# Two orders in a gated linear-attention and S4D kernel: where the output weights are split, and k's sum behind q's clamp

## The chip, the cores and the metric

The kernel runs on one core of one Trainium2 chip. The metric is the device time of one execution in microseconds (us). A core has five engines that run side by side, each through its own queue in order: TensorE (PE, matmuls; its weight loads are listed as PEld), VectorE (DVE), ScalarE (ACT), GpSimd (POOL) and SyncE (SP, which here issues all transfers). They wait for one another by semaphores. SBUF is the on-chip memory of 128 partitions, PSUM the small memory with eight banks into which PE writes.

## The reference

For x of 2048 x 448 it mixes two branches with a gate taken from x. Branch a is linear attention with 16 heads of 28; branch b is a long convolution (an S4D kernel) over the sequence:

```python
g = sigmoid((x * gate_w).sum(-1, keepdims=True))
q, k, v = split(x @ wqkv)                                # 16 heads of 28
phi = lambda t: where(t > 0, t + 1, exp(t)) + 1e-6
kv = einsum("bhsd,bhse->bhde", phi(k), v)
z = phi(k).sum(over s)
o = einsum("bhqd,bhde->bhqe", phi(q), kv) / (einsum("bhqd,bhd->bhq", phi(q), z) + 1e-6)
a = o @ wo
K = 2 * einsum("dn,dnl->dl", C, exp(A * dt * l)).real    # A, C, dt from the parameters
b = causal_conv(x, K) + x * D_skip
out = g * a + (1 - g) * b
```

## The kernel before, in words

The sequence is cut into 16 chunks of 128 rows. The kernel has a head (chunks 0 and 1, while the weights arrive), a main loop over `c` = 1 to 13, a tail for the last two chunks, and a second loop that makes the output chunk by chunk. The order of the instructions on each engine is the order in which the program issues them; nothing reorders them.

Products are made in a form of fp32 that the array takes in one pass (`F32R`), so each operand is split into a high part (a copy that rounds) and a low part (the difference, helper `low`, line 266), and each product is made of high x high, high x low and low x high. The output weights `wo` are split too, in two halves of two column blocks each: one ACT copy makes the high part of a half (L718), two POOL subtractions make the low parts. They are read only in `mrows` (L894), after the main loop.

One pass of the main loop, in the order of PE's work: k's projection of chunk c + 1 (11 matmuls into the bank `k`, or `v0` for c = 2 and 4), the convolution's running sums `v` of one or two earlier chunks (`do_v`, two matmuls each, which read the x tile and `w`), q's projection of chunk c (11 matmuls into the one bank `q`), and `do_g` for chunk c (11 matmuls of phi(k) with x). Around it:

- `split_next`: ACT copies x of chunk c + 2 (L273), POOL makes its low parts (L266, two instructions), `skip` multiplies x by D_skip on POOL (L288).
- k's features of chunk c + 1: two ACT passes (`k_exp`, L418 and L419), DVE's maximum in the bank (`k_max`, L422), ACT's high part (`k_high`, L430), DVE's low part (`k_low`, L437), and DVE's running sum over the chunks `zb` (`k_sum`, L433).
- q's features of chunk c: ACT's exponentials (`q_exp`, L450 to L456), DVE's maximum (`q_max`, L464) and ACT's final sum, which writes `pq` (`q_add`, L468). For chunk 2 alone the clamp is done in two DVE instructions, `q_max` L461 and L462, and the second writes `pq` itself.
- the convolution's rows: `do_w1` (L510), `do_w2` (L515), `v_post` (L525) and `v_add` (L533) on DVE, `v_row` on ACT (L529) and SP.
- `drip` puts the small steps of the S4D preparation (`s4d_prepare`) between them in passes 1 to 5; at c = 5 eight small transposes of its result (L380) run on PE.

Behind the loop, `z_products` (L555) multiplies the collected rows on DVE, then come the features of chunk 15, the sum of `zb` over the partitions on PE (L749 to L751), and from it POOL's first products of the second part (`norm_a`, L766).

The lines at stake in the main loop are these:

```python
        k_low(c + 1)
        k_sum(c + 1)
...
            q_exp(c, project(c, wqh, wql, D + 2, "q"))
            q_max(c)
...
            q_add(c)
        drip(c, 2)
        if c in (NC - 6, NC - 4):
...
        if c == NC - 6:
...
        do_g(c)
```

Of the kernel before, what the change touches and what calls it, by code (L numbers as in the profile page):

```python
# [8 lines left out]
F32R = mybir.dt.float32r  # L9
# [8 lines left out]
D = 448  # L18
# [3 lines left out]
NC = S // P  # L22
J = 4
DJ = D // J
# [155 lines left out]
def gated_mix_kernel(ctx: ExitStack, tc: tile.TileContext, xin, wv_d, wo_d, abc_d, ldt_d, dsk_d,  # L180
                     first_d, tri_d, ident_d, mask_d, gcat_d, sel_d, nabc_d, nldt_d, xrev_d, lag_d, out):
    nc = tc.nc
    PE, ACT, DVE, POOL, SP = nc.tensor, nc.scalar, nc.vector, nc.gpsimd, nc.sync
# [19 lines left out]
    wo = const.tile([DJ, J, D], F32, name="wo")  # L203
# [19 lines left out]
    xs = work.enter_context(tc.tile_pool(name="xs", bufs=LAG + 4))  # L223
# [9 lines left out]
    def load_x(c):  # L233
        xr[c] = pf[:, 4 * D:4 * D + XC] if c == 3 else xp.tile([P, XC], F32, name="xr", tag="xr")
        if c > 1:
            SP.dma_start(out=xr[c], in_=xin[c])
# [28 lines left out]
    def low(eng, o, r, h):  # L265
        eng.tensor_tensor(out=o, in0=r, in1=h.bitcast(F32), op=ALU.subtract)  # L266

    def split_x(c):
        r = xr[c]
        w = xs.tile([P, XW], F32R, name="xw", tag="x")  # L270
        h, l = xh[c], xl[c] = w, w[:, LT:]
        if c > 1:
            ACT.copy(h[:, :XC], r)  # L273
# [13 lines left out]
    def skip(c):  # L287
        POOL.tensor_tensor(out=y[:, c], in0=xr[c][:, NAT:LO], in1=dsk, op=ALU.mult)  # L288
# [4 lines left out]
    def low_rest(c):  # L293
        low(POOL, xh[c][:, XC:LT], xr[c][:, NAT:LO], xh[c][:, NAT:LO])
# [91 lines left out]
    def pieces(c, wh, wl, n, tag):  # L386
        o = ps.tile([P, 512], F32, name=tag, tag=tag)
        h, l = xh[c], xl[c]
        seq = [(h[:, :P], wh[:, 0])]
        lows = [(l[:, :P], wh[:, 0])]  # L390
        for k in range(1, 4):
            xk = slice(k * P, (k + 1) * P)
            seq += [(h[:, xk], wh[:, k]), (h[:, xk], wl[:, k])]
            lows.append((l[:, xk], wh[:, k]))
        seq += lows

        def run(count):
            for _ in range(min(count, len(seq))):
                a, b = seq.pop(0)
                run.n += 1  # L400
                PE.matmul(o[:, :n], lhsT=a, rhs=b, start=run.n == 1, stop=not seq)  # L401
        run.n = 0
        return o, run

    def project(*args, **kw):
        o, run = pieces(*args, **kw)
        run(11)
        return o
# [6 lines left out]
    def k_exp(c, o):  # L415
        e = pke[c] = tp.tile([P, D], F32, name="e", tag="e")
        pks[c] = o[:, :D]
        ACT.activation(e, pks[c], AF.Relu, scale=-1.0)  # L418
        ACT.activation(e, e, AF.Exp, scale=-1.0)  # L419

    def k_max(c):
        DVE.scalar_tensor_tensor(out=pks[c], in0=pks[c], scalar=1.0, in1=pke.pop(c), op0=ALU.add, op1=ALU.max)  # L422
# [5 lines left out]
    def k_high(c):  # L428
        pkh[c] = tp.tile([P, D], F32R, name="pkh", tag="pkh")
        ACT.add(pkh[c], pks[c], 1e-6)  # L430

    def k_sum(c):
        DVE.scalar_tensor_tensor(out=zb, in0=pks[c], scalar=1e-6, in1=zb, op0=ALU.add, op1=ALU.add)  # L433
# [24 lines left out]
    def q_max(c):  # L458
        if 1 < c < QL:
            e = qe.pop(c)  # L460
            DVE.tensor_scalar(out=e, in0=e, scalar1=1.0, scalar2=1e-6, op0=ALU.min, op1=ALU.add)  # L461
            DVE.scalar_tensor_tensor(out=pq[:, c], in0=qs.pop(c), scalar=C1, in1=e, op0=ALU.add, op1=ALU.max)  # L462
            return
        DVE.scalar_tensor_tensor(out=qs[c], in0=qs[c], scalar=1.0, in1=qe.pop(c), op0=ALU.add, op1=ALU.max)  # L464

    def q_add(c):
        if c >= QL or c < 2:
            ACT.add(pq[:, c], qs.pop(c), 1e-6)  # L468
# [39 lines left out]
    def do_w1(c):  # L508
        v = vt[c] = ps.tile([P, 512], F32, name="v", tag="v%d" % (c % 2))[:, :D]
        DVE.scalar_tensor_tensor(out=v, in0=xh[c][:, NAT:LO].bitcast(F32), scalar=-1.0, in1=slope, op0=ALU.mult,  # L510
                                 op1=ALU.mult)

    def do_w2(c):
        w = wt[c] = tp.tile([P, D], F32R, name="w", tag="w")
        DVE.tensor_tensor(out=w, in0=vt[c], in1=xh[c][:, XC:LT].bitcast(F32), op=ALU.add)  # L515

    def do_v(c):
        for n, w in enumerate((xh[c][:, NAT:LO], wt.pop(c))):
            PE.matmul(vt[c], lhsT=tri, rhs=w, start=n == 0, stop=n == 1)  # L519

    def v_post(c):
        t = vt[c]
        if c == NC - 1:
            vt[c] = tp.tile([P, D], F32, name="t", tag="v0")
        DVE.tensor_tensor(out=vt[c], in0=t, in1=near, op=ALU.mult)  # L525

    def v_row(c):
        r = tp.tile([P, D], F32, name="ut", tag="v0")
        ACT.copy(r[96:], vt.pop(c)[96:])  # L529
        SP.dma_start(out=u[c:c + 1], in_=r[P - 1:P])  # L530

    def v_add(c):
        DVE.tensor_tensor(out=y[:, c], in0=y[:, c], in1=vt[c], op=ALU.add)  # L533

    prep = s4d_prepare()
    def steps(n):
        for _ in range(n):
            next(prep, None)
# [3 lines left out]
    def drip(c, i):  # L542
        if (c, i) == (2, 2):
            ACT.copy(tri, trir)
        steps(DRIP.get((c, i), 0))
# [82 lines left out]
    woh, wol = [], []  # L628
    for c in range(1, NC - 2):
        if c == 1:  # L630
            load_x(4)
            gcr = tp.tile([P, D], F32, name="gcr", tag="w")[:KZ, :2 * RX].rearrange("p (g m) -> p g m", g=2)
            for o, i in ((mask, mask_d), (gcr, gcat_d), (sel, sel_d)):
                SP.dma_start(out=o, in_=i)
        elif c + 3 < NC:
            load_x(c + 3)
        if c == 4:
            SP.dma_start(out=wv, in_=wv_d)
            SP.dma_start(out=wo, in_=wo_d)
        ko, k_run = pieces(c + 1, wkh, wkl, D, "v0" if c in (2, 4) else "k")  # L640
        k_run(KA)
        if c == LAG + 2:
            steps(1)
        k_run(11)

        def split_next():
            if c + 2 < NC:
                split_x(c + 2)
                low(POOL, xl[c + 2], xr[c + 2][:, :NAT], xh[c + 2][:, :NAT])
                if c > 1:  # L650
                    low_rest(c + 2)
                    skip(c + 2)

        if c not in (2, LAG + 2):
            split_next()
        drip(c, 0)
        k_exp(c + 1, ko)
        if c == 2:
            split_next()
        if c == 1:  # L660
            skip(1)
            low_rest(2)
            skip(2)
            low_rest(3)
            skip(3)
        now = vq[:]
        for n in now:
            do_v(n)
        for n in now[:1]:
            v_post(n)  # L670
            v_add(n)
        if c == LAG + 2:
            now = [vs.pop(0)]
            do_w1(0)
            do_w2(0)
        k_max(c + 1)
        if c == LAG + 2:
            steps(1)
        drip(c, 1)
        k_high(c + 1)  # L680
        if c == 1:
            for n in range(2):
                q_add(n)
            steps(1)
        for n in now[1:]:
            v_post(n)
        k_low(c + 1)
        k_sum(c + 1)
        for n in now[1:]:
            v_add(n)  # L690
        if c:
            vq = [vs.pop(0) for _ in range(1 + (c + 1 in TWICE))] if c > LAG + 1 else []
        if c > LAG + 2:
            for n in vq:
                do_w1(n)
        if c > 1:
            q_exp(c, project(c, wqh, wql, D + 2, "q"))
            q_max(c)
        if c == LAG + 2:
            do_v(0)  # L700
            split_next()
            v_post(0)
            v_add(0)
            for n in vq:
                do_w1(n)
        if c > LAG + 1:
            for n in vq:
                do_w2(n)
        for n in now:
            v_row(n)  # L710
        if c > 1:
            q_add(c)
        drip(c, 2)
        if c in (NC - 6, NC - 4):
            wos = xs.tile([DJ, 2, 2, D], F32R, name="wos", tag="x")
            woh.append(wos[:, 0])
            wol.append(wos[:, 1])
            ACT.copy(woh[-1], wo[:, 2 * len(woh) - 2:2 * len(woh)])  # L718
        if c == NC - 6:
            for j in range(2):  # L720
                low(POOL, wol[0][:, j], wo[:, j], woh[0][:, j])
        do_g(c)
        if c == LAG:
            POOL.tensor_copy(gcat, gcr)
# [5 lines left out]
    do_v(NC - 1)  # L730
    zr = z_products()
    v_post(NC - 1)
    for j in range(2):
        low(POOL, wol[1][:, j], wo[:, 2 + j], woh[1][:, j])
    POOL.memset(rows[DT:RX, :RG * P], 0.0)
    k_max(NC - 1)
    k_sum(NC - 1)
# [370 lines left out]
```

## Time and profile before

| what | value |
|---|---|
| median of 3 runs | 182.28 us (182.15 to 182.75) |
| the profiled execution | 182.17 us, its span 180.4 us |
| PE busy | 173.8 us (96%) |
| PE weight loads busy | 154.8 us (86%) |
| DVE, ACT, POOL busy | 133.5, 118.8 and 99.6 us (74, 66 and 55%) |
| mean granted TensorE clock | 0.994 |

How to read the lines shown further on. A line of an engine's timeline has the start from the beginning of the span and the duration in us, the engine, the line of the kernel (a helper's own line where a helper issues it), the operation, out<-in by the program's names, shapes and how many instructions were merged into the row; in square brackets stands the idle time before it and the instruction whose end is taken to have ended that. A line of the waits has the waiting instruction, what it waited for, the total in us, how often, and the longest. The chain that ended last is listed as start, duration and what it was. Matmuls overlap: the row of one is longer than the distance to the next. A DVE or POOL instruction that is held back by something other than a semaphore shows as a longer row, not as idle time.

### The profile page before, as it was taken

The numbers are of one execution on the slowest core, as the hardware profiler recorded it, in microseconds if no ns is written. First come the engines' busy times: TensorE is split into PE (matmuls) and PEld (weight loads), VectorE is DVE, ScalarE is ACT, GpSimd is POOL, SyncE is SP. The second block draws the span as 40 slices with busy tenths as digits, with TensorE's granted clock in tenths as the row PEclk, the third lists the DMA queues.
The fourth block names the chain that finished last, engine by engine and source line by source line (L and its number), as shares of the span: only waits on it lengthen the run. The fifth ranks groups of instructions, "written<-read, shape, count | busy, mean of one in ns | idle before, by whom it ended". The sixth has DMA issues, their size and how long they took to land.

```text
span 180.4 us, 2797 instructions
## 1 busy us (share of the span) xinstructions
PE 173.8 (96%) x894; PEld 154.8 (86%) x894; DVE 133.5 (74%) x264; ACT 118.8 (66%) x255; POOL 99.6 (55%) x95
## 2 busy tenths in 40 slices
PE   6999999999999999999999999999999999999991
PEld 6699997998988888898987999979999989899990
DVE  2885358765977799889879789867898798977440
ACT  4799578585756567675586876384675766765630
POOL 1059959852087347173465719739778767864000
PEclk9999999999999999999999999999999999999997
DMA  6999991890011303213030300000001212213222
GB/s 178 339 347 291 226 311 52 340 275 0 0 59 62 117 1 116 68 53 119 0 117 3 122 0 0 8 16 7 1 0 52 106 52 103 102 52 110 102 83 82
DMA packets 8388, 18.37 MB, mean 102 GB/s; under 512 B 1772, under 2 KB 5728, under 8 KB 8144
## 3 DMA queue, kind: packets, MB, share of 16 engines
q1 hardware_dynamic: 8368, 18.14, 31.1%
q8 instruction: 9, 0.15, 0.3%
q14 instruction: 11, 0.09, 0.2%
HBM read 14.28 MB, written 3.67 MB: 100 GB/s over the span
## 4 chain that ended last, share of the span: by engine, by line
PE 59%; DVE 12%; ACT 10%; DMA 9%; issue 4%; SPq 2%; POOL 1%; DVEq 0%
PE a L837 20%; PE q L401 10%; PE g L504 9%; PE k L401 6%; DMA xr<-in 6%; PE tr L815 4%; DMA y<-in 3%; PE v L519 3%; PE m L894 2%; ACT xw L273 2%; DVE v L510 2%; DVE zb L433 2%; SPq L243 2%; ACT pkh L430 2%; DVE k L422 2%
## 5 line engine op out<-in xcount | busy, mean ns | idle before, releaser
L266 POOL TENSOR_TENSOR xw<-xr,xw 128x448 fp32r<-128x448 f32 (+1 forms) x28 | 34.5, 1252 | 37.3 <-ACT xw L273 24.5
L504 PE MATMUL g<-pkh,xw 128*128 128x448 f32 x112 | 35.6, 366 | 0.0
L401 PE MATMUL q<-wqh,xw 128*128 128x450 f32 x112 | 32.4, 369 | 0.4 <-DVE pq L462 0.4
L401 PE MATMUL k<-wkh,xw 128*128 128x448 f32 x96 | 27.6, 368 | 0.0
L837 PE MATMUL a<-wkh,th 128*128 128x448 f32 (+1 forms) x119 | 26.9, 365 | 0.0
L504 PE MATMUL g<-pkl,xw 128*128 128x448 f32 x64 | 23.5, 367 | 0.0
L504 PEld LDWEIGHTS g<-pkh,xw 128*128 128x128 f32 x112 | 21.1, 188 | 2.6
L401 PEld LDWEIGHTS q<-wqh,xw 128*128 128x128 f32 x112 | 20.9, 188 | 2.5 <-ACT xw L273 0.8
L837 PEld LDWEIGHTS a<-wkh,th 128*128 128x128 f32 x119 | 20.6, 190 | 1.3
L766 POOL TENSOR_TENSOR prod<-pq,zb 128x448 f32<-128x448 f32 x16 | 18.6, 1164 | 4.0 <-ACT zb L752 3.1
L787 POOL TENSOR_TENSOR pn<-pq,den 128x448 f32<-128x448 f32 x16 | 15.1, 945 | 9.9 <-DVE den L778 7.3
L401 PEld LDWEIGHTS k<-wkh,xw 128*128 128x128 f32 x96 | 17.9, 188 | 1.9 <-issue 0.3
L288 POOL TENSOR_TENSOR y<-xr,rows 128x448 f32<-128x448 f32 x15 | 17.5, 1165 | 0.0
L273 ACT CAST xw<-xr 128x1024 fp32r<-128x1024 f32 x13 | 13.6, 1044 | 3.2 <-PE v L519 1.7
L401 PE MATMUL q<-wql,xw 128*128 128x450 f32 x42 | 15.5, 368 | 0.0
L842 DVE SCALAR_TENSOR_TENSOR ot<-y,og,a 128x448 f32<-128x448 f32 (+1 forms) x17 | 10.5, 619 | 6.7 <-PE a L837 6.6
L819 ACT CAST th<-tr 128x512 fp32r<-128x512 f32 x16 | 9.4, 587 | 8.7 <-PE tr L815 8.5
L468 ACT ACTIVATE pq<-q 128x448 f32<-128x448 f32 x13 | 7.1, 545 | 12.0 <-DVE q L464 10.4
L820 DVE TENSOR_TENSOR th<-tr,th 128x512 fp32r<-128x512 f32 x16 | 11.0, 686 | 4.0 <-ACT th L819 3.9
L430 ACT ACTIVATE pkh<-k 128x448 fp32r<-128x448 f32 x13 | 7.1, 544 | 10.0 <-DVE k L422 7.7
L510 DVE SCALAR_TENSOR_TENSOR v<-xw,rows 128x448 f32<-128x448 f32 x16 | 10.8, 703 | 3.3 <-ACT ru L382 2.1
L401 PE MATMUL k<-wkl,xw 128*128 128x448 f32 x36 | 13.2, 367 | 0.0
(184 smaller groups left out, 372.7 us busy)
## 6 DMA issues: line engine op xcount, KB each, us to landing
xr<-in SPq DMA_DIRECT2D x13, 512.0 KB, 4.9
out<-ot SPq DMA_DIRECT2D x15, 224.0 KB, 1.9
pq<-in SPq DMA_DIRECT2D x2, 896.0 KB
y<-in SPq DMA_DIRECT2D x4, 225.0 KB
wv<-in SPq DMA_DIRECT2D x1, 896.0 KB
wo<-in SPq DMA_DIRECT2D x1, 784.0 KB
y<-in SPq DMA_DIRECT2D x3, 224.0 KB, 4.2
xr<-in SPq DMA_DIRECT2D x2, 256.0 KB
```

Source lines behind the costliest of these rows:

```text
L266: eng.tensor_tensor(out=o, in0=r, in1=h.bitcast(F32), op=ALU.subtract)
L273: ACT.copy(h[:, :XC], r)
L288: POOL.tensor_tensor(out=y[:, c], in0=xr[c][:, NAT:LO], in1=dsk, op=ALU.mult)
L401: PE.matmul(o[:, :n], lhsT=a, rhs=b, start=run.n == 1, stop=not seq)
L430: ACT.add(pkh[c], pks[c], 1e-6)
L504: PE.matmul(g[i][:a.shape[1], :D], lhsT=a, rhs=b, start=c == 0 and n == 0, stop=c == NC - 1 and end)
L510: DVE.scalar_tensor_tensor(out=v, in0=xh[c][:, NAT:LO].bitcast(F32), scalar=-1.0, in1=slope, op0=ALU.mult, op1=ALU.mult)
L766: POOL.tensor_tensor(out=pd[c], in0=pq[:, c], in1=zb, op=ALU.mult)
L787: POOL.tensor_tensor(out=hd(n[:, :D]), in0=hd(pq[:, c]), in1=dn[c // 2][:, c % 2, :, None].to_broadcast([P, H, DH]), op=ALU.mult)
L820: DVE.tensor_tensor(out=l, in0=ov, in1=h.bitcast(F32), op=ALU.subtract)
L837: PE.matmul(a[:, lo:hi], lhsT=u_, rhs=w_[:, lo:hi], start=n == 0, stop=n == 10)
L842: DVE.scalar_tensor_tensor(out=ot[:, lo:hi], in0=y[:, c, lo:hi], scalar=og[:, c:c + 1], in1=a[:, lo:hi], op0=ALU.mult, op1=ALU.add)
```

## The change

Two orders are changed; no instruction is added or removed.

- In pass c = 2, `k_sum` of chunk 3 is issued behind `q_max` of chunk 2 instead of ahead of q's projection. On DVE, that is one instruction (L433) behind two (L461, L462).
- In passes c = 10 and c = 12, the split of a half of the output weights is issued between q's exponentials (with q's maximum and the rows of v behind them) and `q_add`, instead of behind `q_add`. On ACT the copy comes ahead of L468. On POOL the two subtractions of the first half stay in pass 10; those of the second half move from behind the loop into pass 12, ahead of the subtractions of x of chunk 15 and its skip product.

```diff
--- before.py
+++ after.py
@@ -685,7 +685,8 @@
         for n in now[1:]:
             v_post(n)
         k_low(c + 1)
-        k_sum(c + 1)
+        if c != 2:
+            k_sum(c + 1)
         for n in now[1:]:
             v_add(n)
         if c:
@@ -696,6 +697,8 @@
         if c > 1:
             q_exp(c, project(c, wqh, wql, D + 2, "q"))
             q_max(c)
+        if c == 2:
+            k_sum(c + 1)
         if c == LAG + 2:
             do_v(0)
             split_next()
@@ -708,17 +711,18 @@
                 do_w2(n)
         for n in now:
             v_row(n)
+        if c in (NC - 6, NC - 4):
+            wos = xs.tile([DJ, 2, 2, D], F32R, name="wos", tag="x")
+            h, l = wos[:, 0], wos[:, 1]
+            r = wo[:, 2 * len(woh):2 * len(woh) + 2]
+            woh.append(h)
+            wol.append(l)
+            ACT.copy(h, r)
+            for j in range(2):
+                low(POOL, l[:, j], r[:, j], h[:, j])
         if c > 1:
             q_add(c)
         drip(c, 2)
-        if c in (NC - 6, NC - 4):
-            wos = xs.tile([DJ, 2, 2, D], F32R, name="wos", tag="x")
-            woh.append(wos[:, 0])
-            wol.append(wos[:, 1])
-            ACT.copy(woh[-1], wo[:, 2 * len(woh) - 2:2 * len(woh)])
-        if c == NC - 6:
-            for j in range(2):
-                low(POOL, wol[0][:, j], wo[:, j], woh[0][:, j])
         do_g(c)
         if c == LAG:
             POOL.tensor_copy(gcat, gcr)
@@ -730,8 +734,6 @@
     do_v(NC - 1)
     zr = z_products()
     v_post(NC - 1)
-    for j in range(2):
-        low(POOL, wol[1][:, j], wo[:, 2 + j], woh[1][:, j])
     POOL.memset(rows[DT:RX, :RG * P], 0.0)
     k_max(NC - 1)
     k_sum(NC - 1)
```

## The prediction

> **What bounds the kernel now.** I read the page's busy shares first, then the chain of waits of the TensorE (PE) alone, then PE's own instructions in order of time around each wait, and last the other engines' instructions in the same stretches. PE is busy almost throughout, so the time is PE's work plus the places where PE stands still. After the first loads there are three, and the changed lines touch all three:
>
> ```profile
> PE q L401 <- DVE pq L462: 0.4, 1, 0.4
> PE v L519 <- ACT pq L468: 0.3, 1, 0.3
> PE k L749 <- DVE pkl L437: 0.2, 1, 0.2
> 37.87 2.26 PE q L401 x11
> ```
>
> The idle figures understate the loss. An undisturbed projection takes 2.26 us for 11 matmuls (last row, from the chain that ended last), so PE's pace is 0.205 us from start to start, while a matmul's row is about 0.37 us long and covers part of a gap. I therefore measure each loss from start to start.
>
> **Stall 1, at 30 us (q's clamp of chunk 2).**
>
> ```profile
> 29.43 0.99 PE L401 MATMUL k<-wkh,xw 128*128 128x448 f32 x4
> 30.86 0.66 PE L401 MATMUL q<-wqh,xw 128*128 128x450 f32 x2 [0.44 <-DVE pq L462]
> 31.36 0.36 PE L401 MATMUL q<-wql,xw 128*128 128x450 f32 x1
> ...
> 28.27 0.61 DVE L433 SCALAR_TENSOR_TENSOR zb<-v,zb 128x448 f32<-128x448 f32 x1
> 28.80 1.19 DVE L461 TENSOR_SCALAR e<-e 128x448 f32<-128x448 f32 x1
> 30.09 0.62 DVE L462 SCALAR_TENSOR_TENSOR pq<-q,e 128x448 f32<-128x448 f32 x1
> 30.63 0.91 DVE L326 SCALAR_TENSOR_TENSOR y<-pq 112x512 f32<-112x512 f32 x1
> ...
> 27.33 1.30 POOL L266 TENSOR_TENSOR xw<-xr,xw 128x512 fp32r<-128x512 f32 x1 [2.26 <-ACT xw L273]
> ...
> 29.69 1.30 POOL L288 TENSOR_TENSOR y<-xr,rows 128x448 f32<-128x448 f32 x1
> 30.95 1.73 POOL L266 TENSOR_TENSOR xw<-xr,xw 128x512 fp32r<-128x512 f32 x1
> ```
>
> From 29.43 to 31.36 PE starts six matmuls; at pace that is 6 x 0.205 = 1.23 us, it took 1.93: the loss is 0.70 us. There is one q bank in PSUM, so q of chunk 3 waits until L462 has read q of chunk 2 (ends 30.71, PE starts 0.15 later). The reader is to see why L462 is late: L461 starts at 28.80 and ends at 29.99, 0.30 after a POOL instruction ended and the next one began (29.69), and that next one is longer than its like. L326 ends at 31.54, 0.55 after the next POOL boundary (30.99), and the POOL instruction there takes 1.73. VectorE (DVE) and POOL exclude each other for these forms, and DVE gets its turn between two POOL instructions.
>
> **The edit at c = 2** puts k's sum (L433, 0.53 us start to start) behind the clamp. L461 then asks at 28.27 instead of 28.80. That is 0.36 us before the first POOL subtraction ends (27.33 + 1.30 = 28.63), where before it came after that and had to sit out the second one. L461 would run 28.63 to 28.93, L462 from 29.03 to 29.65 (the 0.10 between them as now), and PE could start at 29.80. PE's own pace allows 29.43 + 0.82 = 30.25, so the wait is gone with 0.45 us to spare. k's sum follows at 29.6 to 30.2; nobody reads zb before the last chunk, and its bank is next written 5 us later. L326, queued behind it, still gets its turn at the end of POOL's skip product, about 31.0: POOL has given DVE 0.15 us one instruction earlier and nothing later, so L326 ends near 31.54 as now.
>
> What is late next: not all of PE's 0.70 us can pass on.
>
> ```profile
> 29.56 1.05 ACT L273 CAST xw<-xr 128x1024 fp32r<-128x1024 f32 x1 [0.50 <-DMA xr<-in]
> ...
> 32.36 0.54 ACT L430 ACTIVATE pkh<-k 128x448 fp32r<-128x448 f32 x1 [0.70 <-DVE k L422]
> 33.39 0.17 ACT L450 ACTIVATE e<-q 128x1 f32<-128x1 f32 x1 [0.49 <-PE q L401]
> ...
> 43.15 0.77 PEld L380 LDWEIGHTS p<-ident,sm 112*128 112x128 f32 x8 [0.16 <-DVE sm L309]
> ```
>
> The exponentials of q(3) (L450) wait for PE and could come at 32.69, but ScalarE (ACT) holds the pkh of chunk 4 from 32.36 to about 32.80, and that hangs, by way of the x copy at 29.56, on a load and not on PE. So ACT's and DVE's chain moves by 33.39 - 32.80 = about 0.60 us. It carries the small S4D steps whose result the eight transposes at 43.15 already wait for (0.16), so I book 0.60 for this edit. Its bounds: 0.70 if the transposes have slack, 0.05 if that chain does not move at all.
>
> **Stall 2, at 99 us (first half of the output weights, chunk 10).**
>
> ```profile
> 97.78 0.98 PE L401 MATMUL k<-wkh,xw 128*128 128x448 f32 x4
> 99.10 0.44 PE L519 MATMUL v<-xw,tri 128*128 128x448 f32 x1 [0.34 <-ACT pq L468]
> ...
> 99.58 0.57 PE L401 MATMUL q<-wqh,xw 128*128 128x450 f32 x2
> ...
> 96.51 1.39 DVE L510 SCALAR_TENSOR_TENSOR v<-xw,rows 128x448 f32<-128x448 f32 x1
> ...
> 98.34 0.61 DVE L515 TENSOR_TENSOR w<-v,xw 128x448 fp32r<-128x448 f32 x1
> ...
> 91.64 2.28 POOL L266 TENSOR_TENSOR wos<-wo,wos 112x448 fp32r<-112x448 f32 x2 [4.01 <-ACT wos L718]
> ...
> 96.25 1.16 POOL L288 TENSOR_TENSOR y<-xr,rows 128x448 f32<-128x448 f32 x1
> ...
> 87.90 0.95 ACT L529 COPY ut<-v 32x448 f32<-32x448 f32 x2
> 90.19 0.55 ACT L468 ACTIVATE pq<-q 128x448 f32<-128x448 f32 x1 [1.34 <-DVE q L464]
> 90.63 0.93 ACT L718 CAST wos<-wo 112x896 fp32r<-112x896 f32 x1
> 91.46 1.05 ACT L273 CAST xw<-xr 128x1024 fp32r<-128x1024 f32 x1
> ```
>
> 97.78 to 99.58 holds six starts: 1.80 against 1.23, a loss of 0.57 us. The wait is named after ACT's pq, but those matmuls read w, whose L515 ends at 98.95, 0.15 before PE starts. L515 is late because L510, with both inputs in SBUF, sat behind POOL's skip product until 97.41 (1.39 us), and the skip product ran so late because POOL did the output weights' two subtractions first.
>
> The edit puts the 0.93 us copy L718 into the 1.34 us in which ACT waits for q's maximum: it would run 88.85 to 89.78, ahead of pq at 90.19, and costs nothing there as long as that wait covers it. The x copy L273 then starts at 90.63 instead of 91.46, and everything of chunk 12 behind it on ACT is 0.83 us earlier. POOL starts the two subtractions at 89.85 instead of 91.64, in a stretch in which it idled 4.01 us; the next ones, and with them the skip product, end at about 95.65 instead of 97.41. DVE's L510, after maximum, low part and sums (0.4 earlier at least), asks at about 96.1 and finds POOL free. It takes about 0.6, L464 and L515 follow, w is ready at 97.8, and PE's pace asks for it at 98.60. I book the whole 0.57; the lower bound is 0, if something else holds L510.
>
> At chunk 12 the same copy moves in the same way (another 0.9 us off ACT's chain ahead of the x copy of chunk 15). No PE wait stands there now, so I book nothing: it is cover for stall 3.
>
> **Stall 3, at 118 us (second half's subtractions, out of the tail).**
>
> ```profile
> 118.15 0.37 PE L504 MATMUL g<-pkh,xw 128*128 128x448 f32 x1
> ...
> 119.60 0.36 PE L504 MATMUL g<-pkl,xw 128*64 128x448 f32 x1
> ...
> 114.04 1.70 DVE L555 TENSOR_TENSOR ru<-pq,ru 15x448 f32<-15x448 f32 x1 [0.86 <-DMA pq<-ut]
> ...
> 116.20 0.61 DVE L422 SCALAR_TENSOR_TENSOR k<-k,e 128x448 f32<-128x448 f32 x1
> ...
> 118.63 0.62 DVE L266 TENSOR_TENSOR zl<-zb,zh 128x448 fp32r<-128x448 f32 x1
> ...
> 114.64 0.58 ACT L419 ACTIVATE e<-e 128x448 f32<-128x448 f32 x1
> ...
> 113.01 2.26 POOL L266 TENSOR_TENSOR wos<-wo,wos 112x448 fp32r<-112x448 f32 x2
> ```
>
> Between 118.15 and 119.60 PE starts one g matmul, two one-column ones (0.12 together) and two for z: at pace 0.205 + 0.12 + 0.41 = 0.73, it took 1.45, a loss of 0.72 us. Those matmuls wait for pkl and zl of the last chunk. Their chain runs through L555, whose 1.70 us end at 115.74, 0.47 after POOL's second wos subtraction. With both subtractions gone from here, L555 should take 0.5 to 0.6 (what it took after its turn came). The maximum L422 is then held by ACT's exponential (ends 115.22) instead of by L555: about 115.25 instead of 116.20, 0.95 earlier. zl ends near 118.3 against a z matmul due at about 118.7, pkl near 117.75 against 118.35. The wait goes: 0.72 us. POOL's first product of the next stage waits for z, so it moves with PE. Bounds: 0 and 0.72.
>
> In sum 0.60 + 0.57 + 0.72 = 1.89 us. The profiled execution took 182.17 us (span 180.40 and 1.77 around it), 0.11 under the median 182.28. 182.17 - 1.89 = 180.28, on the median's level 180.4.
>
> **A page beside the rows.** The Trainium skill, "SBUF — State Buffer", section "Who interferes with whom", says that a VectorE instruction with two SBUF inputs contends with a GpSimd one that reads SBUF, and that whoever issues first has the shared ports for its whole length. By that rule L555, which asked at 114.04, before POOL's second subtraction, should have run before it and ended near 114.6; the trace has 115.74. So the rule holds for the exclusion and not for the turn: by the rule stall 3 would not be there to win, the sum 1.17 and the time 181.1; by the trace it is.
>
> **Rivals.**
>
> *The clamp misses its turn (first edit worth nothing).* DVE got its turn at 29.69 and at 30.95, but L555 missed one, asking about 0.1 us before it. L461 would ask 0.36 us before 28.63, as L326 did before 30.99 (30.63), and L326 got in. Below some margin between 0.1 and 0.36 it loses: then L461 ends at 29.99 as now and stall 1 stays. A transpose chain that does not move gives the same. 1.29 us are left: 181.0.
>
> *The late edits do nothing, only the first works.* L510 held by another POOL instruction, or L555 by one. Against it: after 112.1 POOL has nothing queued but a memset that waits for DVE. 0.60 left: 181.7, at the edge of no change (a measurement of this kernel tells about 0.3%, 0.55 us).
>
> *Slower: the subtractions, moved forward, hit L510.*
>
> ```profile
> 88.45 1.17 DVE L510 SCALAR_TENSOR_TENSOR v<-xw,rows 128x448 f32<-128x448 f32 x2 [0.40 <-ACT ut L529]
> ```
>
> Two L510 run from 88.45 to 89.62, and POOL would start at 89.85. If it started before the second one (89.0), that would wait out a subtraction, 1.15 us, w would be late and PE would stand for some 0.9 us; chunk 12 has the same pair, so 1.8 in all, with stall 2 kept: 1.8 - 0.60 - 0.72 = +0.5, 182.8. It decides only if the copy, which has to follow both ut copies on ACT (88.85) and take 0.93, ended 0.8 us early; I see nothing that would do that.
>
> **How the numbers follow.** All three stalls gone 0.67 (180.4, from 179.9 to 180.8); first edit worth nothing 0.17 (181.0); late edits worth nothing 0.12 (181.7, most of it inside 0.3%); slower 0.04. Faster by over 0.3%: 0.67 + 0.17 + 0.02 = 0.86; within 0.10; slower 0.04. The range takes in the first two cases: 179.9 to 181.2.
>
> **What would show it.** Right: L461 about 0.6 us long, q's first matmul of chunk 3 directly behind k's; L510 near 0.63 everywhere; L555 near 0.6; PE's list of waits without the three rows above; the x copies of chunks 13 and 15 straight after pq. Wrong: L461 still at 1.2 and the wait on L462 still there; the eight transposes starting much later than 0.6 us before 43.15; a new PE wait on w around 91 or 106 us; or the time saved at 30 us coming back as a longer wait at 68 us, where PE also waits for w.

## The result and the profile after

| | before | changed |
|---|---|---|
| median of 6 runs each, one chip | 182.59 us (182.15 to 183.64) | 180.55 us (180.13 to 181.03) |
| the profiled execution | 182.17 us, span 180.4 us | 180.51 us, span 178.7 us |

The ratio is 0.9882, with a 95% interval of 0.9851 to 0.9914: faster by 1.2%. The forecast was 180.4 us. The ratios here and below leave out runs more than 1.5% above the fastest of their kernel, so they differ a little from the quotients of the medians.

PE's list of waits in the changed kernel has one row left, the one in the head that was there before. The three that the prediction named are gone:

```profile
PE q L305 <- DVE ones_r L228: 1.4, 1, 1.4
```

The first place, in the timeline of the changed kernel (start, duration, instruction):

```profile
29.39 0.99 PE L401 MATMUL k<-wkh,xw 128*128 128x448 f32 x4
30.22 0.58 PE L401 MATMUL q<-wqh,xw 128*128 128x450 f32 x2
...
27.70 0.61 DVE L461 TENSOR_SCALAR e<-e 128x448 f32<-128x448 f32 x1
28.42 0.62 DVE L462 SCALAR_TENSOR_TENSOR pq<-q,e 128x448 f32<-128x448 f32 x1
...
26.77 2.57 POOL L266 TENSOR_TENSOR xw<-xr,xw 128x512 fp32r<-128x512 f32 x2 [1.57 <-ACT xw L273]
...
25.64 1.05 ACT L273 CAST xw<-xr 128x1024 fp32r<-128x1024 f32 x1 [0.47 <-DMA xr<-in]
```

L461 takes 0.61 us instead of 1.19: it asks at 27.70, in the first of POOL's two subtractions, and runs between them. L462 ends at 29.04, and q's first matmul of chunk 3 starts 0.83 us after the first of k's last four, which is 4 x 0.205 with no gap. k's sum (L433) follows at 28.96. The last row matters below: the x copy of chunk 4, which both POOL and DVE follow here, started at 25.64. In the profile of before it started 0.56 later:

```profile
26.20 1.05 ACT L273 CAST xw<-xr 128x1024 fp32r<-128x1024 f32 x1 [0.99 <-DMA xr<-in]
```

The second place, in the timeline of the changed kernel:

```profile
97.08 0.98 PE L401 MATMUL k<-wkh,xw 128*128 128x448 f32 x4
97.90 0.37 PE L519 MATMUL v<-xw,tri 128*128 128x448 f32 x1
98.31 0.57 PE L401 MATMUL q<-wqh,xw 128*128 128x450 f32 x2
...
95.42 0.63 DVE L510 SCALAR_TENSOR_TENSOR v<-xw,rows 128x448 f32<-128x448 f32 x1 [0.40 <-ACT ut L529]
96.50 0.62 DVE L515 TENSOR_TENSOR w<-v,xw 128x448 fp32r<-128x448 f32 x1
...
89.23 2.27 POOL L266 TENSOR_TENSOR wos<-wo,wos 112x448 fp32r<-112x448 f32 x2 [2.25 <-ACT wos L720]
...
88.21 0.94 ACT L720 CAST wos<-wo 112x896 fp32r<-112x896 f32 x1
89.53 0.55 ACT L468 ACTIVATE pq<-q 128x448 f32<-128x448 f32 x1 [0.37 <-DVE q L464]
89.97 1.04 ACT L273 CAST xw<-xr 128x1024 fp32r<-128x1024 f32 x1
```

The copy of the output weights (L718 before, L720 now) sits in the idle time ahead of pq, the x copy follows pq directly, L510 is 0.63 us long instead of 1.39, w is ready at 97.12, and the six starts from 97.08 to 98.31 take 1.23 us, which is the pace.

The third place, the same view:

```profile
116.91 0.37 PE L504 MATMUL g<-pkh,xw 128*128 128x448 f32 x1
117.20 0.19 PE L751 MATMUL k<-oks,ones_r 112*1 112x1 f32 x2
117.32 0.47 PE L752 MATMUL k<-zh,ones_r 128*128 128x448 f32 x1
117.64 0.37 PE L753 MATMUL k<-zl,ones_r 128*128 128x448 f32 x1
117.84 0.37 PE L504 MATMUL g<-pkl,xw 128*64 128x448 f32 x1
...
112.69 0.61 DVE L555 TENSOR_TENSOR ru<-pq,ru 15x448 f32<-15x448 f32 x1 [0.86 <-DMA pq<-ut]
114.01 0.63 DVE L422 SCALAR_TENSOR_TENSOR k<-k,e 128x448 f32<-128x448 f32 x1 [0.16 <-ACT e L419]
116.45 0.61 DVE L266 TENSOR_TENSOR zl<-zb,zh 128x448 fp32r<-128x448 f32 x1
```

L555 takes 0.61 us instead of 1.70, L422 waits for ACT alone, and no wait is left. But from 116.91 to 117.84 PE takes 0.93 us, not the 0.73 that the prediction called its pace.

How PE's starts shifted between the two profiles shows where the time came from: first matmul of k of chunk 5 at 35.46 before and 34.72 after (0.74 earlier), of chunk 13 96.35 and 95.65 (0.70), of chunk 14 104.09 and 102.79 (1.30), of chunk 15 111.61 and 110.37 (1.24), and the g matmul behind z 119.60 and 117.84 (1.76). Three steps, at the three places.

### The profile page after: what moved, and what is told of

Same layout as the page of the kernel before. It is cut to its first block, busy times and chain, and to the rows that moved or that the text cites. A ratio compares the mean times of both kernels' runs of the same rounds, so it can differ in the third digit from the quotient of the medians.

```text
span 178.7 us, 2800 instructions
## 1 busy us (share of the span) xinstructions
PE 173.2 (97%) x894; PEld 155.6 (87%) x894; DVE 132.8 (74%) x264; ACT 119.3 (67%) x255; POOL 99.4 (56%) x95
## 4 chain that ended last, share of the span: by engine, by line
PE 93%; DVE 3%; ACT 2%; issue 0%
PE a L839 20%; PE g L504 19%; PE q L401 16%; PE k L401 14%; PE tr L817 4%; PE v L519 4%; PE v L569 3%; PE v L401 3%; PE m L896 2%; PE q L305 2%; PE k L569 2%; PE q L569 1%; PE k L859 1%; PE tr L859 1%; DVE v L510 1%; ACT xw L273 1%
## 5 line engine op out<-in xcount | busy, mean ns | idle before, releaser
L468 ACT ACTIVATE pq<-q 128x448 f32<-128x448 f32 x13 | 7.1, 545 | 9.3 <-DVE q L464 8.1
L510 DVE SCALAR_TENSOR_TENSOR v<-xw,rows 128x448 f32<-128x448 f32 x16 | 10.1, 655 | 4.0 <-ACT ru L382 2.1
```

## The experiments

The times of one kernel spread widely (the kernel before from 181.22 to 184.83 us beside the first four experiments), and the traces show differences in the head. So each experiment is read in two ways: by its ratio, and by PE's way in its profile, the time from the first matmul of `do_g` of chunk 2 (about 26 us) to the last matmul, against that in the profile of before. The theory: each of the three edits removes its own wait by the mechanism of the prediction, and the gains add. The main rivals: the early copies alone do it; a wait comes back later; the gain at 30 us is not the edit's.

**The three edits one at a time.** A: only k's sum moved, on the kernel before:

```diff
-        k_sum(c + 1)
+        if c != 2:
+            k_sum(c + 1)
...
+        if c == 2:
+            k_sum(c + 1)
```

> The kernel before with k's sum of chunk 3 behind the clamp of chunk 2, and nothing else. Theory (each edit frees a wait of PE of its own, and nothing later eats it): the clamp's first half is 0.6 us long instead of 1.19, q of chunk 3 follows k directly, PE is 0.70 us earlier from there to the end, the two later waits stay; span 179.7, ratio 0.996. Rival 1 (the saving comes back as a longer wait at 68 us, where PE waits for w): PE earlier at 35 us, not after 70 us; span 180.4, ratio 1. Rival 2 (the clamp misses its turn between two POOL instructions): the clamp's first half stays near 1.2 us, ratio 1.

Measured: 181.95 us against 182.59, ratio 0.9977 (0.9944 to 1.0010). PE's way is 0.64 us shorter. Two of the rows of PE's waits, and the timeline of this kernel:

```profile
PE v L519 <- ACT pq L468: 0.3, 1, 0.3
PE k L752 <- DVE pkl L437: 0.2, 1, 0.2
```

```profile
29.89 0.99 PE L401 MATMUL k<-wkh,xw 128*128 128x448 f32 x4
30.71 0.58 PE L401 MATMUL q<-wqh,xw 128*128 128x450 f32 x2
...
28.15 0.61 DVE L461 TENSOR_SCALAR e<-e 128x448 f32<-128x448 f32 x1
28.86 0.62 DVE L462 SCALAR_TENSOR_TENSOR pq<-q,e 128x448 f32<-128x448 f32 x1
...
26.08 1.05 ACT L273 CAST xw<-xr 128x1024 fp32r<-128x1024 f32 x1 [0.42 <-DMA xr<-in]
```

The first wait is gone and the other two stand. What PE won at 30 us is not given back later. But the 0.64 us are not the edit's worth: the x copy of chunk 4 started at nearly the same time as in the profile of before (26.20), while PE itself was 0.46 us later (29.89 against 29.43), so PE had more time to spare here. The table behind G gives the old order a loss of only 0.04 us in this execution.

B: only the first half of the output weights moved, copy and subtractions of pass 10 ahead of `q_add`:

```diff
+        if c == NC - 6:
+            split_wo(True)      # the ACT copy and the two POOL subtractions
         if c > 1:
             q_add(c)
         drip(c, 2)
...
+        if c == NC - 4:
+            split_wo(False)     # the ACT copy alone; its subtractions behind the loop
```

> The kernel before with the first half of the output weights (copy and both subtractions) ahead of q's final sum in pass 10, the second half as before. Theory: POOL's skip product of chunk 13 ends 1.8 us earlier, do_w1 of chunk 12 takes 0.63 us instead of 1.39, the wait at 99 us goes, PE 0.57 us earlier from there, the wait at 118 us stays; span 179.8, ratio 0.997. Rival (this wait and the one at 118 us are one chain, so the saving at 99 us only lengthens the wait at 118 us): the wait there grows by 0.5 us, ratio 1.

Measured: 181.82 us, ratio 0.9975 (0.9936 to 1.0014). L510 of chunk 12 starts at 96.43 and takes 0.63 us, the wait at 99 us is gone, and PE's way gets 0.58 us shorter there. The wait at 118 us stands. The first wait stands too, and is larger than in the profile of before:

```profile
PE q L401 <- DVE pq L462: 0.8, 1, 0.8
```

```profile
26.57 1.05 ACT L273 CAST xw<-xr 128x1024 fp32r<-128x1024 f32 x1 [1.30 <-DMA xr<-in]
...
30.47 0.62 DVE L462 SCALAR_TENSOR_TENSOR pq<-q,e 128x448 f32<-128x448 f32 x1
```

Nothing was changed there; the copy started 0.37 later than in the profile of before (26.20), L462 ended 0.38 later.

C: only the second half moved, copy and subtractions into pass 12 ahead of `q_add`:

```diff
+        if c == NC - 4:
+            split_wo(True)
         if c > 1:
             q_add(c)
         drip(c, 2)
         if c == NC - 6:
...
+            split_wo(True)
...
-    for j in range(2):
-        low(POOL, wol[1][:, j], wo[:, 2 + j], woh[1][:, j])
```

> The kernel before with the second half of the output weights (copy and both subtractions) ahead of q's final sum in pass 12, the first half as before. Theory: the wait at 99 us stays, the product behind the loop (L555) takes 0.6 us instead of 1.70, the wait at 118 us goes: 0.5 us, as the two traces measured, rather than the 0.72 of the prediction; span 179.9, ratio 0.997. Rival (the earlier chain has to be freed first): the wait at 118 us stays, ratio 1.

Measured: 182.47 us, ratio 0.9979 (0.9945 to 1.0014). The wait at 99 us stays (0.4), L555 takes 0.61 us, and the wait at 118 us is gone: the stretch that took 1.45 us takes 0.93, which is 0.52 less, and 0.44 of that are left at the end of PE's way. At 30 us this execution has no wait at all, with the old order:

```profile
29.35 0.99 PE L401 MATMUL k<-wkh,xw 128*128 128x448 f32 x4
30.18 0.61 PE L401 MATMUL q<-wqh,xw 128*128 128x450 f32 x2
...
25.45 1.05 ACT L273 CAST xw<-xr 128x1024 fp32r<-128x1024 f32 x1 [0.32 <-DMA xr<-in]
```

Its x copy started 0.75 us earlier than in the profile of before, and PE's way is 0.65 us shorter there, as much as in A, without the edit.

The two late edits, 0.58 + 0.44 us, and the 0.64 us by which the way of A is shorter come to 1.66 us, as much as the whole change takes out of PE's way (1.61 to 1.73 in its first profile and in F and J below). So the gains at the three places add in PE's rows, whatever the cause of the first. The timed runs are too spread to say it: none of the three ratios is clear of no change, and their product, 0.9931, lies above the 0.9882 and 0.9911 (H below) of the whole.

**What in the two late edits does it.** D: the subtractions of the second half in pass 12, but the copies left behind `q_add`:

```diff
+        if c == NC - 4:
+            for j in range(2):
+                low(POOL, wol[1][:, j], wo[:, 2 + j], woh[1][:, j])
...
-    for j in range(2):
-        low(POOL, wol[1][:, j], wo[:, 2 + j], woh[1][:, j])
```

> As the run with the second half alone, but its ACT copy stays behind q's final sum; only the two POOL subtractions move from behind the loop into pass 12. Theory (it needs both): the subtractions start after the copy, at about 106.6 us, push the skip product of chunk 15 to 111.3 to 112.5 us, where do_w1 of chunk 15 asks for SBUF at 111.5 us and is held for about 1 us; w comes late and PE gets a new wait of about 0.4 us at 114 us, while the one at 118 us goes: some 0.1 to 0.2 us won, ratio 0.999 to 1. Rival (only the subtractions' absence behind the loop counts, the copy's place is without effect): as with the whole second half, ratio 0.997.

Measured: 181.90 us, ratio 0.9972 (0.9942 to 1.0002). The timeline:

```profile
110.96 1.38 DVE L510 SCALAR_TENSOR_TENSOR v<-xw,rows 128x448 f32<-128x448 f32 x1
...
110.69 1.16 POOL L288 TENSOR_TENSOR y<-xr,rows 128x448 f32<-128x448 f32 x1
```

The wait at 118 us is gone, but POOL's skip product of chunk 15 now comes late enough to hold L510 of that chunk, and PE loses 0.27 us at the running sum of chunk 15 (its matmul at 113.54 starts 0.39 us after the one before, instead of 0.20). Net 0.23 us at this end instead of 0.44. The subtractions moved without the copy set up stall 2 a second time.

E: the reverse for the first half, copy where it was, subtractions moved behind the loop:

```diff
         if c == NC - 6:
-            for j in range(2):
-                low(POOL, wol[0][:, j], wo[:, j], woh[0][:, j])
...
     POOL.memset(rows[DT:RX, :RG * P], 0.0)
+    for j in range(2):
+        low(POOL, wol[0][:, j], wo[:, j], woh[0][:, j])
```

> The kernel before with the first half's two POOL subtractions moved to the end of POOL's work ahead of the second part (behind the memset of rows); its ACT copy stays behind q's final sum, as does all of the second half. Theory (POOL's lateness is what holds do_w1 at 96.5 us): the skip product of chunk 13 ends near 96.2 us, do_w1 of chunk 12 takes 0.63 us instead of 1.39, the 0.57 us at 99 us go, the wait at 118 us stays. Rival (ACT's copy, 0.93 us ahead of the x copy, is what makes w late): do_w1 is short, but the wait at 99 us stays at half its length or more.

Measured: 182.97 us against 182.21, ratio 1.0034 (0.9999 to 1.0069). At 99 us it goes as expected: ACT's copy is in its old place, POOL is free, L510 takes 0.63 us and the wait is gone (0.58 us). So POOL holding DVE is the cause there, not ACT's order by itself. At 118 us the expectation was wrong; the wait did not stay as it was but grew by 0.9 us:

```profile
114.42 1.72 DVE L555 TENSOR_TENSOR ru<-pq,ru 15x448 f32<-15x448 f32 x1 [0.86 <-DMA pq<-ut]
...
119.03 1.54 DVE L266 TENSOR_TENSOR zl<-zb,zh 128x448 fp32r<-128x448 f32 x1
...
113.39 2.28 POOL L266 TENSOR_TENSOR wos<-wo,wos 112x448 fp32r<-112x448 f32 x2
...
117.83 2.26 POOL L266 TENSOR_TENSOR wos<-wo,wos 112x448 fp32r<-112x448 f32 x2
```

zl, 0.61 us long when free, sat out a subtraction and PE waited 0.9 us for it. The hazard is a subtraction of that size, wherever it is put, beside a DVE instruction on PE's path that POOL can hold: zl and L555 read both their inputs from SBUF. L437, which reads one from PSUM, asked at 118.49 in the middle of the same subtraction and took its usual 0.62 us.

F: the changed kernel with the second half's subtractions put back behind the loop, the copies left early:

```diff
+            if c == NC - 6:
                 for j in range(2):
                     low(POOL, l[:, j], r[:, j], h[:, j])
...
+    for j in range(2):
+        low(POOL, wol[1][:, j], wo[:, 2 + j], woh[1][:, j])
```

> The changed kernel, but the second half's two subtractions back behind the loop; both copies stay early. Theory (the copy's early place moves all of POOL's later work 1.3 us ahead): the subtractions run at 111.0 to 113.3 us, the product behind the loop asks at 112.7 us, is held until 113.3 and ends near 113.8, only 0.35 us late, and that is within the slack: at most 0.15 us slower than the changed kernel. Rival (the subtractions must leave that place): the wait at 118 us is back, 0.45 us slower than the changed kernel.

Measured: 180.77 us, ratio 0.9928 (0.9892 to 0.9965), PE's way 1.73 us shorter than before's, like the changed kernel's.

```profile
112.98 0.95 DVE L555 TENSOR_TENSOR ru<-pq,ru 15x448 f32<-15x448 f32 x1 [0.85 <-DMA pq<-ut]
...
111.17 2.28 POOL L266 TENSOR_TENSOR wos<-wo,wos 112x448 fp32r<-112x448 f32 x2
...
29.76 0.99 PE L401 MATMUL k<-wkh,xw 128*128 128x448 f32 x4
30.59 0.58 PE L401 MATMUL q<-wqh,xw 128*128 128x450 f32 x2
...
26.60 1.05 ACT L273 CAST xw<-xr 128x1024 fp32r<-128x1024 f32 x1 [1.05 <-DMA xr<-in]
```

The subtractions need not leave the tail: with the copies early, POOL is through with them at 113.45 instead of 115.27, while PE is 1.3 us earlier, and L555 loses 0.3 us instead of 1.1, which the chain has to spare. The last three rows are the first place: q follows k without a gap, though the x copy of chunk 4 started later than in the profile of before.

**The clamp: POOL's hold or the load.** G: on the kernel before, the second low part and the skip product of chunk 4 are issued a pass later, behind the first low part of chunk 5, so that POOL has two instructions fewer beside the clamp; DVE's order is the old one:

```diff
-                if c > 1:
+                if c == 3:
+                    low_rest(c + 1)
+                    skip(c + 1)
+                if c > 2:
                     low_rest(c + 2)
                     skip(c + 2)
```

> The kernel before, DVE's order unchanged (k's sum ahead of the clamp), but POOL's second subtraction and skip product of chunk 4 are put behind its first subtraction of chunk 5, so that POOL is idle when the clamp asks. In the runs so far the clamp's second half ended 4.51 us after the start of the x copy of chunk 4 with the old order (four runs) and 3.40 us after it with the new one (two runs). Theory (0.53 us of the 1.11 are k's sum, the rest is the wait for POOL): the clamp's first half takes 0.4 us and the second half ends 3.7 us after that copy's start, so the wait at 30 us is gone here too where the load does not land later than about 26.4 us. Rival (DVE's order alone): 4.5 us after it, and the wait is as long as in the kernel before at the same landing.

```profile
28.53 0.38 DVE L461 TENSOR_SCALAR e<-e 128x448 f32<-128x448 f32 x1
29.01 0.62 DVE L462 SCALAR_TENSOR_TENSOR pq<-q,e 128x448 f32<-128x448 f32 x1
...
25.93 1.05 ACT L273 CAST xw<-xr 128x1024 fp32r<-128x1024 f32 x1 [0.72 <-DMA xr<-in]
```

L461 takes 0.38 us, its duration with POOL out of the way, and PE has no wait at 30 us (0.68 us won there, the whole way 0.61 us shorter). So 0.8 us of L461's 1.19 were POOL. The median did not move (182.15 against 182.21, ratio 1.0004, 0.9974 to 1.0033), and one profile cannot say why.

The executions differ in when the x copy of chunk 4 starts. From that start to L462's end it is 4.51 to 4.54 us in all six profiles with the old order and POOL's old place (before, B, C, D, E, and I below), and 3.40 us in all six with the new order (after, A, F, and H, J and K below); in G it is 3.70. So the edit takes 1.11 us out of this chain. What PE feels of it depends on how far ahead of PE's own work the copy starts; call the time from the copy's start to the first of k's last four matmuls its lead. Undisturbed, q starts 0.82 us after the first of k's last four matmuls; where PE waited for L462, q started 0.15 us after its end. So the old order is in time when the lead is at least 4.51 + 0.15 - 0.82 = 3.84 us, and the new one when it is 2.73 us. PE's loss is how much later than 0.82 us q started; the last column is 3.84 less the lead, that is what the old order would lose at this lead.

| profile | order on DVE | lead of the copy, us | PE's loss, us | old order by the sum, us |
|---|---|---|---|---|
| before | old | 3.23 | 0.61 | 0.61 |
| B | old | 2.92 | 0.92 | 0.92 |
| C | old | 3.90 | 0 | 0 |
| D | old | 3.78 | 0.06 | 0.06 |
| E | old | 2.67 | 1.19 | 1.17 |
| I (load issued early) | old | 4.31 | 0 | 0 |
| G (POOL's work later) | old | 3.49 | 0 | 0.35 |
| after | new | 3.75 | 0 | 0.09 |
| A | new | 3.80 | 0 | 0.04 |
| F | new | 3.16 | 0 | 0.68 |
| K | new | 3.36 | 0 | 0.48 |
| J (load issued early) | new | 3.69 | 0 | 0.15 |
| H | new | 2.64 | 0.09 | 1.20 |

The sum gives the loss of every profile of the old order to within 0.02 us. So the edit's worth at 30 us is 0.04 to 1.1 us, by execution; it shows in F, K and H, and hardly in A and in the first profile after. Over the five profiles of the old order with the load in its old place the loss is 0.56 us on average.

H: the changed kernel run again, with nothing altered:

> The changed kernel once more, beside the two runs with the earlier load. Theory: the clamp's second half ends 3.40 us after the start of the x copy of chunk 4 wherever that falls, PE shows none of its three waits, and PE's way from 27 us to the end is as long as in the first profile of this kernel, within 0.1 us; what differs from the first profile lies before 27 us.

Measured: median 180.53 us, ratio 0.9911 (0.9879 to 0.9943). The profiled execution happened to be one of the two longest of twelve: 182.31 us, where ten lie between 180.32 and 180.79. Its PE waits and timeline:

```profile
PE k L401 <- ACT xw L273: 0.4, 1, 0.4
```

```profile
30.75 0.62 DVE L462 SCALAR_TENSOR_TENSOR pq<-q,e 128x448 f32<-128x448 f32 x1
...
27.97 1.05 ACT L273 CAST xw<-xr 128x1024 fp32r<-128x1024 f32 x1 [2.26 <-DMA xr<-in]
```

The load came 2.33 us later than in the first profile. L462 ends 3.40 us after the copy's start, as said ahead, but PE now waits for the x copy itself and its way is 1.15 us longer than in the first profile; the expectation of an equal way failed. From 59 us on the two profiles of the changed kernel run alike, with no wait at 99 or 118 us.

Why the load comes when it does is only hinted at in the windows of 20 to 24 us. The DMA engines are busy all the time (share 1.00 to 1.01) in the profiles of before, of after and of this run, but move 240, 276 and 209 GB/s, and the copies start at 26.20, 25.64 and 27.97. That looks like a backlog that drains at a different rate in each execution. But the rate in this window does not settle it: in E the engines move 265 GB/s and the copy starts at 27.22, in C 255 GB/s and 25.45. What sets the landing is open.

If the load were the matter, issuing it earlier should help. I and J: on the kernel before and on the changed kernel, x of chunk 4 is loaded into columns of `y` that are free by then, right behind the loads of the small constants:

```diff
-        xr[c] = pf[:, 4 * D:4 * D + XC] if c == 3 else xp.tile([P, XC], F32, name="xr", tag="xr")
+        xr[c] = pf[:, 4 * D:4 * D + XC] if c == 3 else yf[:, 2 * XC:3 * XC] if c == 4 else xp.tile([P, XC], F32, name="xr", tag="xr")
...
+    load_x(4)
```

> The kernel before with every engine's compute order unchanged; only the load of x for chunk 4 goes into a place of its own and is issued right behind the S4D loads, some 3.5 us earlier. Theory (the wait at 30 us is set by when that load lands: the clamp's second half ends 4.51 us after the start of the x copy of chunk 4, and PE asks for it at about 30.1): the x copy starts at 25.3 us or somewhat before, the wait at 30 us is gone without the clamp's edit, the waits at 99 and 118 us stay; ratio about 0.996. Rival (the wait comes from DVE's order alone): a PE wait of 0.3 us or more on the clamp is still there.

> The changed kernel with the same earlier load of x for chunk 4. Theory (with the new order the clamp is in time for any landing up to about 26.7 us): no difference to the changed kernel where its load lands before that, so within 0.2% of it; a gain only in executions in which the load comes late. Rival (the head is bound by that load in other ways too): faster than the changed kernel by 0.3% or more.

Measured: 182.31 us on the kernel before, ratio 0.9998 (0.9963 to 1.0033); 180.92 us on the changed kernel, 0.9934 (0.9904 to 0.9963), no better than the changed kernel as it is. The x copy of chunk 4 in I:

```profile
24.80 1.03 ACT L274 CAST xw<-y 128x1024 fp32r<-128x1024 f32 x1
```

In I, ACT took the copy without a wait and the stall at 30 us was gone in that profile; in J, ACT still waited 0.53 us for the load and the copy started at 25.76. The expected gain on the median of I did not come, and its times spread from 181.14 to 183.44 us all the same. So an earlier issue does not make the head steady, and whether the spread of the times comes from this load alone or from others in the head was not settled.

**An attempt to go further.** PE still loses about 0.25 us at 57.0 and 0.43 at 67.2 in the changed kernel. K: in passes 6 and 7 of the changed kernel, k's exponentials were put ahead of `split_next`, as pass 2 has them:

```diff
-        if c not in (2, LAG + 2):
+        if c not in (2, 6, 7, LAG + 2):
             split_next()
...
-        if c == 2:
+        if c in (2, 6, 7):
             split_next()
```

> The changed kernel, and in passes 6 and 7 ACT makes k's two exponentials ahead of the copy of x, which there waits for PE's running sums (1.03 and 0.63 us). Theory (PE's remaining losses in the loop, 0.25 us at 57.0 us behind the k bank and 0.43 us at 67.2 us behind w, hang on that copy): k's maximum comes 0.9 to 1.2 us earlier in both passes, the two losses go, up to 0.6 us faster than the changed kernel, ratio to the kernel before 0.985. Rival (the copy of x, now 0.9 us later, makes the x parts late for k's projection of the next pass): a new PE wait in passes 7 or 8, no gain.

Measured: 180.95 us, ratio 0.9917 (0.9882 to 0.9952). The loss at 57 us is gone and 0.29 us of the one at 67, but PE loses 0.7 us at 60, and its way is 0.15 us longer than the changed kernel's. The timeline:

```profile
60.02 0.47 PE L519 MATMUL v<-xw,tri 128*128 128x448 f32 x1 [0.31 <-DVE w L515]
...
56.50 2.41 DVE L510 SCALAR_TENSOR_TENSOR v<-xw,rows 128x448 f32<-128x448 f32 x2
...
56.88 1.54 POOL L288 TENSOR_TENSOR y<-xr,rows 128x448 f32<-128x448 f32 x1
```

The later split puts POOL's skip product beside L510 (two take 2.41 us, in the changed kernel 1.23), and w is late. It is stall 2 at a new place. No version tried beat the changed kernel.

## Why the prediction was right, step by step

*The clamp.* The mechanism held: L461 got its turn with a margin of about 0.3 us in each of the six profiles that have the new order, and G shows that POOL was what held it. The size, 0.60 us, was worked out from one execution, as if its landing were a constant. By the table the loss of the old order runs from 0 to 1.19 us; that 0.60 lies near the mean of the five, 0.56, is luck as far as the working goes. In the first profile after, the copy came early, and there the old order would have lost 0.09 us: nearly all of the 0.66 us between these two profiles at 30 us is the landing, and so it is in A. What the edit buys is 1.11 us of the chain. F shows it: its copy had a lead of 3.16 us, and PE has no wait where the old order would lose 0.68. When the load comes later still, the changed kernel pays as well (H: 1.15 us of PE's way, most of it in front of k, which waits for the copy itself). By the timed runs the clamp's edit alone is not clear of no change (A). That the eight transposes would move along was right (43.15 to 42.47), but the bound argued from the pkh of chunk 4 "that hangs on a load" was not put to the test, because the load itself moved.

*The first half of the weights.* Everything came as worked out. With the 0.68 us taken off that PE is earlier by then, the prediction has the copy at 88.17, POOL's subtractions at 89.17, the x copy at 89.95, L510 at 95.4 and w at 97.12; the profile has 88.21, 89.23, 89.97, 95.42 and 97.12. Loss removed: 0.57 booked, 0.57 in the rows, 0.58 in B alone. That L510 would be "near 0.63 everywhere" is nearly so: the median of sixteen is 634 ns, one takes 957.

*The second half.* L422 and zl came as forecast (with the 1.24 us taken off that PE is earlier by chunk 15: L422 at 114.01, measured 114.01; zl ends at 117.06, measured 117.06). The term was still too large: 0.72 booked, 1.45 - 0.93 = 0.52 in these rows and in C's, and 0.44 of it left at the end of PE's way in C. The step that failed is "at pace 0.205 + 0.12 + 0.41 = 0.73": around the one-column matmuls PE starts 0.29 and 0.32 us apart with no wait in sight, so about 0.2 us of what I called a loss is the pace of that sequence. The upper bound of the term, 0.72, could not be reached. F shows also that the reason given, subtractions gone from the tail, is one way and not the only one: with the copies early they may stay. D shows the reverse, subtractions moved without the copy, to be worth half.

*The sum.* 1.89 us were forecast for the median; between the two profiles it is 1.66 (182.17 to 180.51), between the medians of the six runs 2.04. The excess of the second over the first is larger than either step's error. Executions of the old order that met a later load than the profiled one did would explain it: B and E show such executions, with waits of 0.8 and 1.0 us at 30 us; but for the timed runs, which have no trace, that is argued and not shown. The mean loss of the old order at 30 us and the two late gains, 0.56 + 0.58 + 0.44 = 1.58 us or 0.9%, lie within the intervals of both timings of the changed kernel. That the forecast, 180.4, came so near 180.55 is partly luck: the third term was too large by 0.20, and the kernel before was 0.31 slower in six runs than in the three that the forecast started from.

*The rivals.* That the clamp misses its turn: not in six profiles. That the late edits do nothing: ruled out by the profiles of B and C. That the gain at 30 us is not the edit's: true of the first profile after and of A, not of F, K and H. That the moved subtractions make POOL hit L510: not in the changed kernel (its one long L510, 0.96 us at 50.08, is as long in the profile of before), but L510 was hit in D and K, from other moves and by the skip product. The time did not come back at 68 us.

*The rule beside the rows.* By the Trainium skill, "SBUF — State Buffer", section "Who interferes with whom", a VectorE instruction that issues ahead of POOL's next one has the shared ports. E goes against it once more: L555 asked there at 114.42, about 0.1 us before POOL's second subtraction (the middle of 113.39 to 115.67 is 114.53), and took 1.72 us. An instruction in G goes with it: L326 asked at 34.60, as short a time before POOL's next one at 34.68, and ran at once (0.68 us), while that POOL instruction took 1.63 us instead of 1.15.

## What to carry to other kernels

A DVE instruction whose row is twice as long as its like is a wait that no list of waits shows; look for the POOL instruction that spans it, and ask which earlier step on ACT made POOL late. Before moving POOL work, list the DVE instructions on PE's path that it will land beside: three of the moves tried here (D, E, K) made a new meeting, for 0.3 to 0.9 us of PE each. And in a stretch that follows a load, one profile gives one landing: measure how far ahead of the waiting engine's own work it comes, not where it falls in the span, and repeat the profile before booking a wait's size or crediting an edit with its absence.

## What the runs showed of the hardware

When DVE gets in between two POOL instructions that run back to back: it got in when it asked 0.3 us or more before the boundary (L461 at 27.70 for about 28.05, L326 in the profile of before at 30.63 for 30.95), and L555 missed at 0.1 us or so in six profiles (before, A, B, E, G and I; in before at 114.04 for about 114.14, in E at 114.42 for about 114.53). But L326 in G asked at 34.60 for about 34.70 and got in, so the time of asking alone does not decide it; what else does is open. The wait that PE shows as 0.34 us idle cost it 0.57 from start to start. And the transfers of the changed kernel moved 276 GB/s in one execution and 209 in another in the same four microseconds, with the DMA engines busy throughout.
